# Other tables of places for the steps between the matmuls of a fused attention and bilinear GLU kernel

## The chip, the cores and the metric

The kernel runs on one core of one Trainium2 chip, in one launch. The metric is the device time of that launch in microseconds (us). Inputs are float32 in device memory, the output is float32.

## The reference

`x` is 2048 rows of 576 values. Attention has 32 heads of 18 values and a sliding window of 256 keys; the feed-forward part is a bilinear GLU of width 4608, whose output goes through a silu and gates the attention's output.

```python
xn = _layernorm(x)                                   # S = 2048, D = 576
q, k, v = split(xn @ wqkv)                           # H = 32 heads, Dh = 18
scores = einsum("bhqd,bhkd->bhqk", q, k) * Dh ** -0.5
scores = where((i - j >= 0) & (i - j < 256), scores, -1e9)
s = einsum("bhqk,bhkd->bhqd", softmax(scores), v).reshape(B, S, D) @ wo
h = (xn @ w_gate) * (xn @ w_up)                      # F = 4608, no nonlinearity
g = silu(h @ w_down)
return x + s * g
```

## The kernel before

**Numbers in two parts.** Every float32 operand of a matmul is held as two float16 tiles, a hi part and a low part (what the hi part leaves over, scaled), and a product is three matmuls: hi by hi, hi by low, low by hi. Most of the work between the matmuls is the making of these parts: ScalarE writes the hi part (`hi`, L190), VectorE the low part (`lo`, L193).

**Slots.** After a prologue (layer norm, the projections to q, k and v) the kernel runs 72 slots: 18 groups of 256 feed-forward columns, times 4 chunks of 512 rows. A slot is named by its group and chunk, so a group is four slots, and its first slot is the one that begins with new weights. In a slot TensorE computes the up and gate products of its chunk and group in a scheme of seven products of half blocks (`seven_place`, matmuls L1159 and L1112). Four of the seven use differences of weight blocks, which GpSimd makes (`t_sum`, L507, tile tf) and whose parts ScalarE and VectorE make (`t_hi`, `t_lo`, tile tw). The seven results are joined in tiles gt by ScalarE (`seven_copy`, L1125) and VectorE (`seven_add`, L1129), multiplied (`seven_mult`, L1134, on GpSimd for the first half, on VectorE for the second), and split into parts hh (`h_hi`, L1001, ScalarE; `h_lo`, L1007, VectorE). The down product of a slot (`down`, L1023, five of them, 0 to 4, each with a sum into acc on VectorE, L1030) runs in the slot after it, and takes six matmuls: for each half of h, hi by hi, hi by low, low by a copy of the down weight's hi part scaled down (`dn_low`, L605).

**Attention.** The slots from 1 to 64 carry one attention step each: two heads and four blocks of 128 queries (8 pairs of head and block, numbered 0 to 7; a block is 2i and 2i+1). Its stages are `score_pairs` (PE, L896), `score` (VectorE, L907, adds the mask and takes the maximum), `shifted` and `probs` (ScalarE, L915, L919; the second head's also copies the hi parts of P of both heads, L922), `turn_probs` (the low part of P, L928, on GpSimd or VectorE; the second head's then starts the DMA that transposes the block, L931, on SyncE's queue), `weigh` (PE, L940, the products with V), `finish` (VectorE, L952 and L953) and `finish2` (GpSimd, L960, L967, L968), then `store_o`.

**What sets the order.** A slot has 16 places. `seven_place` issues the up and gate matmuls of each; every other step is put by hand with `at(slot, place, f, ...)`, and a place of 16 or more means a place of the next slot. Within a place the scores' matmuls come first, down products second, the rest in the order in which the program puts it there. Each engine runs its steps in this order, so a step that waits holds up what stands behind it on its engine. All the places stand in one dictionary, `AT` (lines 68 to 106); the steps' code doesn't change. Its entries:

- `p`: for each slot of a group, for each of the 8 pairs, the places of score, shifted, probs, turn_probs and weigh. `end`: finish, finish2, store_o. `load`: the loads of k, q, v.
- `en`: for each slot of a group, from the third entry on, the engine of the low part of P of each pair (0 GpSimd, 1 VectorE). `eng`: of its entries two are read by steps, [4] (`dn_low`: 1 ScalarE, 0 GpSimd) and [5].
- `h`: the places of h_hi and h_lo for the two halves. `down`: the five down products. `dn`: parts of the down weights (hi, low, low copy).
- `raw`, `amax`, `scale`: loads and scales of the weights of a group; `up_hi`, `up_lo`, `wd`, `sum`, `t_hi`, `t_lo`: their parts and differences, counted from four slots ahead of the group (so 64 is place 0 of its first slot).
- `sx`, `on`, `t0`, `u0`, `g0`, `wd0`: the same kinds of steps for the first group, and sums of x, in the prologue and slot 0.

```python
(nc.gpsimd, nc.vector)[AT["en"][(s + 1) % NCH][2 + 2 * i + j]].tensor_tensor(...)   # turn_probs, L928
at(sl, AT["h"][sl % NCH][1][ft], h_lo, sl, ft)
at(sl + 1, AT["down"][(sl + 1) % NCH][n], down, sl, n)
```

Of the kernel before, what the change touches and what calls it, by code (L numbers as in the profile page):

```python
# [20 lines left out]
def kernel(  # L21
# [23 lines left out]
    scale = DH ** -0.5  # L45
# [19 lines left out]
    C_OUT = 1.0 / (XS * PROJ * WTOP * WTOP)  # L65
    LEAST, MOST = 2.0 ** -60, 2.0 ** 60

    AT = {"amax": (19, 20, 6),
           "dn": ((41, 45), (51, 52), (52, 48)),
           "down": ((6, 9, 12, 15, 20), (6, 8, 11, 14, 16), (6, 8, 11, 14, 16), (6, 9, 12, 15, 19)),  # L70
           "en": ((0, 1, 0, 0, 0, 0, 1, 0, 0, 0), (0, 1, 0, 0, 0, 0, 1, 0, 0, 0),
                  (0, 1, 0, 0, 0, 0, 1, 0, 0, 0), (0, 1, 0, 0, 0, 0, 1, 0, 0, 0)),
           "end": ((30, 32, 35), (28, 32, 33), (28, 32, 33), (28, 32, 33)),
           "eng": (1, 1, 0, 1, 1, 0, 1, 0, 0, 0, 0, 0, 0, 1),
           "g0": (-22, -19, -22, -21, -9, -16, -14, -11, -11),
           "h": (((15, 17), (18, 21)), ((15, 17), (19, 21)), ((15, 17), (21, 21)), ((15, 17), (19, 21))),
           "load": (8, 3, 15),
           "mult": {1: 6, 4: 18, 5: 1, 6: 0},
# [12 lines left out]
           "pairs": (6, 13),  # L91
           "raw": (8, 9, 12, 16, -6, 0),
           "scale": (26, 28, 35, 51),
           "sum": ((30, 36, 50, 59, 64), (41, 53, 56, 61, 62)),
# [5 lines left out]
           "t_hi": ((57, 57), (67, 69)),  # L100
           "t_lo": ((57, 58), (70, 71)),
           "u0": ((-9, -8, -7, -7), (-7, -7, -7, -4)),
           "up_hi": (36, 36, 60, 61),
           "up_lo": (41, 40, 65, 62),
           "wd": ((55, 56), (65, 69), (70, 74)),
           "wd0": ((-4, 3), (-1, 4), (-1, 7))}

    ctx.enter_context(tc.manual_schedule())
    const = ctx.enter_context(tc.tile_pool(name="const", bufs=1))
# [492 lines left out]
    def dn_low(g, k):  # L602
        w = DW[g, k]
        if AT["eng"][4]:
            nc.scalar.activation(w[:, 2], w[:, 0], AF.Copy, scale=1.0 / LO)  # L605
# [22 lines left out]
    def at(slot, place, f, *a):  # L628
        todo.setdefault(slot * 16 + place, []).append((f, a))
# [5 lines left out]
    for c in range(NCH):  # L635
        steps = s_steps(c)
        for n, f in enumerate(steps):
            for k, f in enumerate(f if isinstance(f, tuple) else (f,)):
                at(0, AT["sx"][c][n] + k, f, (nc.gpsimd, nc.vector)[AT["on"][c][n]])
    for k in range(3):  # L640
        at(0, AT["g0"][k], ffn_amax, 0, (2, 0, 1)[k])
    for k, f in enumerate((ffn_spread_out, ffn_spread_in, ffn_scale, ffn_scale2)):
        at(0, AT["g0"][5 + k], f, 0)
    for kind in range(2):
        for n in range(4):
            at(0, AT["t0"][kind][n], t_sum, 0, kind, n)
        for pair in range(2):
            at(0, AT["t0"][kind][4 + pair], t_hi, 0, kind, pair)
            at(0, AT["t0"][kind][6 + pair], t_lo, 0, kind, pair)
# [675 lines left out]
```

## Time and profile before

| | us |
|---|---|
| device time, median of 3 runs | 1578.68 |
| lowest and highest | 1578.66, 1579.19 |
| the profiled execution's own time | 1580.56 |
| its span in the trace | 1578.8 |
| granted clock of TensorE, mean | 0.999 of full speed |

| engine | busy us | share of the span |
|---|---|---|
| PE (TensorE matmul) | 1556.4 | 99% |
| DVE (VectorE) | 1268.3 | 80% |
| ACT (ScalarE) | 1069.4 | 68% |
| POOL (GpSimd) | 847.7 | 54% |

In the rows below, PE is TensorE's matmul, DVE VectorE, ACT ScalarE, POOL GpSimd. A row of a timeline has the start, the duration, the engine, the line, the operation and the tiles (out<-in) with partitions x elements; x6 at its end joins six instructions that follow each other, and a bracket names the idle time before it and what ended it. A duration runs from an instruction's start to its end, and holds what it waited for after its start. Successive rows of one engine overlap a little, since the next begins in the pipeline behind the one before; the net time of a step is the distance to the next row's start.

### The profile page before, as it was taken

Reading aid. Unit: us, or ns where it says so; the run is one execution under the profiler, and the core shown is the slowest. Engines: PE = TensorE matmul, PEld = TensorE weight load, DVE = VectorE, ACT = ScalarE, POOL = GpSimd, SP = SyncE. Lnnn points to the kernel's source line nnn. Section 1 sums busy time; section 2 is a strip of 40 time slices with the busy share of each in tenths; the row PEclk is TensorE's granted clock in tenths of the full one; section 3 lists DMA queues with packets and bytes.
Section 4 is the critical chain, followed back from the end, with each engine's and each line's share of the span. In section 5 each row is a group of like instructions: output and inputs, shape, how many; then the busy total and the mean of one; then the engine's idle time right before and its main releaser. Section 6 shows DMA issues by size and latency. Waiting matters only on the chain.

```text
span 1578.8 us, 40055 instructions
## 1 busy us (share of the span) xinstructions
PE 1556.4 (99%) x15498; PEld 1106.7 (70%) x15498; DVE 1268.3 (80%) x2752; ACT 1069.4 (68%) x1853; POOL 847.7 (54%) x1064
## 2 busy tenths in 40 slices
PE   8999999999999999999999999999999999999999
PEld 5465577777777776777777777777777777777767
DVE  7537688888888988898889888888888888877654
ACT  6435478777777877777778787878777777752230
POOL 4126355657464757575766666566757575732000
PEclk9999999999999999999999999999999999999999
DMA  9583436565557687777777676767686868651238
GB/s 233 190 246 129 166 73 138 96 129 107 122 106 143 122 146 137 130 143 135 145 122 152 121 155 119 154 121 149 118 158 123 155 120 149 122 98 38 63 82 220
DMA packets 566575, 212.14 MB, mean 134 GB/s; under 512 B 504560, under 2 KB 544624, under 8 KB 566384
## 3 DMA queue, kind: packets, MB, share of 16 engines
q1 hardware_dynamic: 566384, 209.58, 64.2%
q8 instruction: 121, 1.98, 0.6%
q14 instruction: 70, 0.57, 0.1%
HBM read 76.63 MB, written 29.00 MB: 67 GB/s over the span
## 4 chain that ended last, share of the span: by engine, by line
PE 83%; DVE 6%; POOL 4%; DMA 3%; ACT 2%; issue 2%; SPq 1%; DVEq 0%; POOLq 0%; ACTq 0%
PE up L1159 40%; PE dn L1023 21%; PE s L387 4%; PE pv L940 3%; PE up L1112 3%; PE s L896 2%; PE s L1023 2%; PE s L1262 2%; DMA pt<-pp 2%; PE up L1262 2%; PE up L387 1%; POOL pp L928 1%; DVE hh L1007 1%; POOL tf L507 1%; PE s L338 1%
## 5 line engine op out<-in xcount | busy, mean ns | idle before, releaser
L1023 PE MATMUL dn<-dnw,hh 128*128 128x512 f16 (+1 forms) x3168 | 444.7, 286 | 1.2
L1159 PEld LDWEIGHTS <-tw 128*128 128x128 f16 x3456 | 320.2, 98 | 62.1 <-DVE tw L193 5.1
L1023 PEld LDWEIGHTS <-hh 128*128 128x128 f16 x3456 | 222.2, 98 | 170.8 <-issue 19.2
L1159 PEld LDWEIGHTS <-upw 128*128 128x128 f16 x3024 | 283.8, 98 | 64.5 <-issue 22.2
L1129 DVE SCALAR_TENSOR_TENSOR gt<-up,gt 128x512 f32<-128x512 f32 x360 | 247.7, 688 | 62.4 <-PE up L1112 40.3
L1030 DVE SCALAR_TENSOR_TENSOR acc<-dn,sc,acc 128x512 f32<-128x512 f32 x310 | 215.3, 694 | 99.2 <-PE dn L1023 99.0
L1159 PE MATMUL up<-XT,upw 128*128 128x256 f16 x2160 | 276.6, 273 | 0.0
L915 ACT ACTIVATE mx<-mx,sig 128x2 f32<-128x2 f32 x256 | 98.1, 383 | 217.5 <-DVE mx L907 217.5
L1159 PE MATMUL up<-XT,tw 128*128 128x256 f16 x1728 | 236.0, 273 | 2.5 <-DVE gt L1129 2.5
L1159 PE MATMUL up<-sx,tw 128*128 128x256 f16 x1728 | 225.0, 273 | 2.4 <-DVE tw L193 2.4
L1134 POOL TENSOR_TENSOR ht<-gt 128x512 f32<-128x512 f32 x72 | 92.0, 1278 | 94.7 <-DVE gt L1129 93.9
L940 PEld LDWEIGHTS <-pt 128*128 128x128 f16 x2880 | 109.5, 96 | 41.1 <-DMA pt<-pp 6.3
L940 PE MATMUL pv<-vt,pt 128*128 128x37 f16 x2880 | 112.9, 179 | 4.5 <-DMA pt<-pp 4.5
L1159 PE MATMUL up<-sx,upw 128*128 128x256 f16 x864 | 112.7, 273 | 0.0
L1125 ACT ACTIVATE gt<-up 128x512 f32<-128x512 f32 x144 | 83.7, 581 | 30.9 <-PE up L1159 17.3
L1001 ACT ACTIVATE hh<-ht 128x512 f16<-128x512 f32 x72 | 45.2, 627 | 67.4 <-POOL ht L1134 67.4
L507 POOL TENSOR_TENSOR tf<-raw 128x256 f32<-128x256 f32 x102 | 83.0, 814 | 0.1
L507 POOL TENSOR_TENSOR tf<-raw,tf 128x256 f32<-128x256 f32 x68 | 62.0, 913 | 21.8 <-DVE tw L193 21.8
L193 DVE SCALAR_TENSOR_TENSOR upw<-raw,sc,upw 128x640 f16<-128x640 f32 x72 | 71.9, 1001 | 0.0
L315 ACT ACTIVATE upw<-raw 128x1280 bf16<-128x1280 f32 (+1 forms) x51 | 62.5, 1225 | 3.8 <-DMA raw<-in_B_w_up_dram 3.7
L193 DVE SCALAR_TENSOR_TENSOR tw<-tf,sc,tw 128x512 f16<-128x512 f32 x68 | 49.5, 749 | 14.5 <-ACT tw L190 13.7
L896 PE MATMUL s<-ks,qs 54*128 54x384 f16 (+2 forms) x512 | 60.2, 312 | 0.0
(1353 smaller groups left out, 2918.3 us busy)
## 6 DMA issues: line engine op xcount, KB each, us to landing
raw<-in_B_w_down_dram SPq DMA_DIRECT2D x36, 288.0 KB
qk_d<-qp SPq DMA_DIRECT2D x18, 512.0 KB
raw<-in_B_w_gate_dram SPq DMA_DIRECT2D x36, 256.0 KB
raw<-in_B_w_up_dram SPq DMA_DIRECT2D x36, 256.0 KB
ks<-qk_d SPq DMA_DIRECT2D x96, 81.0 KB
qs<-qk_d SPq DMA_DIRECT2D x128, 54.0 KB
vt<-v_d SPq DMA_DIRECT2D x48, 111.0 KB
qk_d<-qp SPq DMA_DIRECT2D x20, 256.0 KB
```

The lines of the kernel that those rows point to most:

```text
L193: nc.vector.scalar_tensor_tensor(w, rv, s, h, op0=OP.mult, op1=OP.subtract)
L387: nc.tensor.matmul(ps, a, b, start=i == 0 and not opened, stop=i == 12 and opened)
L507: nc.gpsimd.tensor_tensor(t[:, to], x0, x1, op=OP.subtract)
L896: nc.tensor.matmul(ps[:, :hi_ - lo_], QS[s][r, i * 128:(i + 1) * 128], KS[s][r, lo_:hi_], start=True, stop=True)
L915: nc.scalar.activation(mx[:, 1], mx[:, 0], AF.Identity, bias=sig[:, 2:3], scale=sig[:, 1:2])
L940: nc.tensor.matmul(PVB[s][:, j, i, :VW], pt[:, nb * j + n + n // nb * nb], VT[s][:, lo_ + n % nb, j * VW:(j + 1) * VW], start=n == 0, stop ...
L1023: nc.tensor.matmul(to, a, b, start=q == 0, stop=q == len(l) - 1)
L1030: nc.vector.scalar_tensor_tensor(d, src, SC[g][:, 9:10], d, op0=OP.mult, op1=OP.add)
L1125: nc.scalar.activation(seven_new(sl, name), CH[q], AF.Copy, scale=H_SC)
L1129: nc.vector.scalar_tensor_tensor(seven_new(sl, name), CH[q], H_SC, x, op0=OP.mult, op1=OP.add)
L1134: eng.tensor_tensor(HT[sl, f], u[:, 0], u[:, 1], op=OP.mult)
L1159: nc.tensor.matmul(CH[q][:, o], a, b, start=CH["first"], stop=last and q not in (1, 2, 5), skip_group_check=q in ON)
```

## The change

Only the tables change; each step computes what it did.

- The low part of P of pair 5 goes from GpSimd to VectorE in three of four slots (`en`, kinds 1 to 3: 48 instructions of 128x384). In slots of kind 0 pairs 4 and 5 change engines with each other.
- `dn_low` (36 instructions of 128x576) goes from ScalarE to GpSimd (`eng[4]`).
- `p` has a table of its own for each kind of slot: in kind 0 the first products with V stand up to three places earlier and those of pairs 4 and 5 one later, in kind 1 the products with V of pairs 2 to 7 two places later; low parts of P of pairs 4 and 5 in kind 2 one place earlier; `probs` of pairs 6 and 7 in kind 3 one place later, so in place 5 of a group's first slot.
- In a group's first slot, where steps of the slot before it spill: the fifth down product at place 2 and not 3 (`down` of kind 3: 18 for 19); `h_lo` of the first half at place 5 and not 3 (`h` of kind 3: 21 for 19), behind the small low part of `wd` that comes there from place 6; `t_hi` of the first pair at place 5 and not 3, behind `probs`. The fifth down product of kind 0 moves the other way, to place 5 of the second slot.
- `h`, `dn`, `sum`, `t_lo`, `up_hi`, `scale`, `load`, `raw`, `end` shift by one to seven places; steps of the prologue (`sx`, `on`, `t0`, `u0`, `g0`, `wd0`) shift, and three of its sums change engine.

```diff
--- before.py
+++ after.py
@@ -65,45 +65,45 @@
     C_OUT = 1.0 / (XS * PROJ * WTOP * WTOP)
     LEAST, MOST = 2.0 ** -60, 2.0 ** 60
 
-    AT = {"amax": (19, 20, 6),
-           "dn": ((41, 45), (51, 52), (52, 48)),
-           "down": ((6, 9, 12, 15, 20), (6, 8, 11, 14, 16), (6, 8, 11, 14, 16), (6, 9, 12, 15, 19)),
-           "en": ((0, 1, 0, 0, 0, 0, 1, 0, 0, 0), (0, 1, 0, 0, 0, 0, 1, 0, 0, 0),
-                  (0, 1, 0, 0, 0, 0, 1, 0, 0, 0), (0, 1, 0, 0, 0, 0, 1, 0, 0, 0)),
-           "end": ((30, 32, 35), (28, 32, 33), (28, 32, 33), (28, 32, 33)),
-           "eng": (1, 1, 0, 1, 1, 0, 1, 0, 0, 0, 0, 0, 0, 1),
-           "g0": (-22, -19, -22, -21, -9, -16, -14, -11, -11),
-           "h": (((15, 17), (18, 21)), ((15, 17), (19, 21)), ((15, 17), (21, 21)), ((15, 17), (19, 21))),
-           "load": (8, 3, 15),
-           "mult": {1: 6, 4: 18, 5: 1, 6: 0},
-           "on": ((0, 0, 0, 0, 1, 0, 1, 1, 1, 0, 0, 0, 0, 0, 1, 0, 1),
+    AT = {"amax": (18, 20, 6),
+           "dn": ((41, 45), (51, 55), (52, 48)),
+           "down": ((6, 9, 12, 15, 21), (6, 8, 11, 14, 16), (6, 8, 11, 14, 16), (6, 9, 12, 15, 18)),
+           "en": ((0, 1, 0, 0, 0, 0, 0, 1, 0, 0), (0, 1, 0, 0, 0, 0, 1, 1, 0, 0),
+                  (0, 1, 0, 0, 0, 0, 1, 1, 0, 0), (0, 1, 0, 0, 0, 0, 1, 1, 0, 0)),
+           "end": ((29, 31, 32), (30, 33, 35), (28, 32, 35), (28, 30, 33)),
+           "eng": (1, 1, 0, 0, 0, 0, 1, 0, 0, 0, 1, 0, 1, 1),
+           "g0": (-22, -21, -20, -18, -10, -17, -14, -11, -11),
+           "h": (((15, 17), (18, 19)), ((15, 19), (19, 21)), ((15, 17), (18, 21)), ((15, 17), (21, 21))),
+           "load": (7, 3, 13),
+           "mult": {1: 6, 4: 20, 5: 1, 6: 0},
+           "on": ((0, 0, 0, 1, 0, 0, 0, 1, 1, 0, 0, 0, 1, 0, 1, 0, 1),
                   (0, 1, 0, 1, 0, 0, 0, 1, 0, 0, 1, 0, 1, 1, 0, 0, 0),
-                  (1, 0, 0, 1, 0, 0, 1, 1, 1, 0, 1, 0, 1, 1, 1, 1, 1),
-                  (0, 0, 1, 0, 0, 1, 0, 0, 0, 0, 1, 1, 1, 1, 0, 0, 1)),
-           "p": (((6, 7, 8, 11, 22), (6, 7, 8, 12, 22), (7, 8, 12, 13, 22), (7, 8, 12, 13, 23),
-                  (13, 14, 15, 18, 24), (13, 14, 15, 19, 24), (13, 15, 20, 21, 30), (15, 17, 20, 21, 30)),
+                  (1, 0, 0, 1, 0, 0, 1, 1, 1, 0, 1, 0, 1, 1, 1, 0, 1),
+                  (0, 0, 1, 0, 0, 1, 1, 0, 0, 0, 1, 1, 0, 1, 0, 0, 0)),
+           "p": (((6, 7, 8, 10, 19), (6, 7, 9, 12, 20), (7, 8, 12, 13, 21), (7, 8, 12, 13, 22),
+                  (13, 14, 15, 18, 25), (13, 14, 15, 19, 25), (13, 15, 20, 21, 29), (15, 17, 20, 21, 29)),
+                 ((6, 7, 8, 11, 22), (6, 7, 8, 12, 22), (7, 8, 10, 13, 24), (7, 8, 10, 13, 25),
+                  (13, 14, 15, 18, 26), (13, 14, 15, 19, 26), (13, 15, 20, 21, 30), (15, 17, 20, 21, 30)),
+                 ((6, 7, 8, 11, 22), (6, 7, 8, 12, 22), (7, 8, 12, 14, 22), (7, 8, 12, 14, 23),
+                  (13, 14, 15, 16, 25), (13, 14, 15, 18, 25), (13, 15, 20, 21, 28), (15, 17, 20, 21, 28)),
                  ((6, 7, 8, 11, 22), (6, 7, 8, 12, 22), (7, 8, 12, 13, 22), (7, 8, 12, 13, 23),
-                  (13, 14, 15, 18, 24), (13, 14, 15, 19, 24), (13, 15, 20, 21, 28), (15, 17, 20, 21, 28)),
-                 ((6, 7, 8, 11, 22), (6, 7, 8, 12, 22), (7, 8, 12, 13, 22), (7, 8, 12, 13, 23),
-                  (13, 14, 15, 17, 26), (13, 14, 15, 19, 26), (13, 15, 20, 21, 28), (15, 17, 20, 21, 28)),
-                 ((6, 7, 8, 11, 22), (6, 7, 8, 12, 22), (7, 8, 12, 13, 22), (7, 8, 12, 13, 23),
-                  (13, 14, 15, 19, 26), (13, 14, 15, 20, 26), (13, 15, 20, 22, 28), (15, 17, 20, 22, 28))),
+                  (13, 14, 15, 19, 26), (13, 14, 15, 20, 26), (13, 15, 21, 22, 28), (15, 17, 21, 22, 28))),
            "pairs": (6, 13),
-           "raw": (8, 9, 12, 16, -6, 0),
-           "scale": (26, 28, 35, 51),
-           "sum": ((30, 36, 50, 59, 64), (41, 53, 56, 61, 62)),
+           "raw": (7, 9, 16, 17, -6, -2),
+           "scale": (26, 28, 35, 50),
+           "sum": ((32, 39, 46, 59, 66), (43, 53, 56, 61, 62)),
            "sx": ((-24, -24, -24, -23, -22, -22, -18, -18, -17, -17, -14, -13, -13, -19, -18, -17, -14),
                   (-20, -20, -20, -18, -17, -16, -16, -16, -16, -15, -13, -13, -9, -15, -15, -15, -12),
                   (-13, -11, -11, -9, -7, -7, -3, -3, 2, 3, 4, 5, 6, 4, 6, 7, 14),
-                  (-4, -1, -1, 6, 8, 9, 11, 12, 14, 15, 16, 16, 24, 23, 26, 26, 26)),
-           "t0": ((-19, -9, -7, -7, -6, -2, -5, -1), (-11, -8, -4, -7, -4, -2, -1, -1)),
-           "t_hi": ((57, 57), (67, 69)),
-           "t_lo": ((57, 58), (70, 71)),
-           "u0": ((-9, -8, -7, -7), (-7, -7, -7, -4)),
-           "up_hi": (36, 36, 60, 61),
+                  (-4, -1, -1, 6, 8, 9, 11, 12, 14, 15, 16, 19, 24, 23, 26, 26, 26)),
+           "t0": ((-14, -10, -8, -7, -6, -2, -5, -1), (-10, -8, -4, -6, -4, -2, -1, -1)),
+           "t_hi": ((57, 57), (69, 70)),
+           "t_lo": ((57, 57), (70, 71)),
+           "u0": ((-8, -7, -7, -3), (-7, -7, -6, -1)),
+           "up_hi": (37, 37, 61, 61),
            "up_lo": (41, 40, 65, 62),
-           "wd": ((55, 56), (65, 69), (70, 74)),
-           "wd0": ((-4, 3), (-1, 4), (-1, 7))}
+           "wd": ((55, 56), (65, 71), (69, 74)),
+           "wd0": ((-2, 2), (-1, 4), (-1, 7))}
 
     ctx.enter_context(tc.manual_schedule())
     const = ctx.enter_context(tc.tile_pool(name="const", bufs=1))
```

## Rows read from the trace of the kernel before

**Rows 1.** The page: busy us of TensorE, and its granted clock in tenths.

```profile
PE 1556.4 (99%) x15498; PEld 1106.7 (70%) x15498; DVE 1268.3 (80%) x2752; ACT 1069.4 (68%) x1853; POOL 847.7 (54%) x1064
PEclk9999999999999999999999999999999999999999
```

**Rows 2.** Windows: stretch, busy us of each engine (instructions), clock, DMA share, GB/s.

```profile
493.00:1403.00 910.00, 901.91 (x9803) 656.20 (x9802) 786.96 (x1723) 711.53 (x1199) 586.04 (x709) 1.00 0.73 136
```

**Rows 3.** Chain of waits in order of time: start us, us, what.

```profile
493.40 1.64 PE up L1159 x15
...
1024.99 1.64 PE up L1159 x15
...
1043.64 1.64 PE up L1159 x15
...
1100.57 1.54 PE up L1159 x14
...
1402.99 1.64 PE up L1159 x15
```

**Rows 4.** Waits of TensorE: line, releaser, us in total, times, longest.

```profile
PE pv L940 <- DMA pt<-pp: 4.5, 5, 1.1
PE up L1159 <- DVE gt L1129: 2.5, 2, 2.1
PE up L1159 <- DVE tw L193: 2.4, 8, 0.4
```

**Rows 5.** Timeline of TensorE, first slot of a group.

```profile
1076.29 1.75 PE L1023 MATMUL dn<-dnw,hh 128*128 128x512 f16 x6
```

**Rows 6.** Timeline of VectorE, the same slot.

```profile
1074.11 0.48 DVE L1030 SCALAR_TENSOR_TENSOR acc<-dn,sc,acc 128x256 f32<-128x256 f32 x1 [0.27 <-PE dn L1023]
1074.51 1.12 DVE L928 TENSOR_TENSOR pp<-sm__17355,pp 128x384 f16<-128x384 f32 x1
1075.55 1.40 DVE L1007 SCALAR_TENSOR_TENSOR hh<-hh,ht 128x512 f16<-128x512 f16 x1
1076.87 0.68 DVE L1007 SCALAR_TENSOR_TENSOR hh<-hh,gt 128x512 f16<-128x512 f16 x1
```

**Rows 7.** Timeline of GpSimd, the same slot.

```profile
1074.08 0.45 POOL L968 TENSOR_TENSOR ob<-o,ob 128x144 f16<-128x144 f32 x1
1074.49 0.73 POOL L507 TENSOR_TENSOR tf<-raw 128x256 f32<-128x256 f32 x1
1075.17 1.23 POOL L928 TENSOR_TENSOR pp<-sm__17355,pp 128x384 f16<-128x384 f32 x1
```

**Rows 8.** Timeline of ScalarE, the same slot.

```profile
1075.25 0.72 ACT L190 ACTIVATE tw<-tf,sc 128x512 f16<-128x512 f32 x1 [0.69 <-POOL tf L507]
1075.88 1.29 ACT L919 ACTIVATE sm__17359<-sm__17359,mx,sig 128x384 f32<-128x384 f32 x2
1077.20 0.83 ACT L922 CAST pp<-sm__17359 128x768 f16<-128x768 f32 x1
```

**Rows 9.** Groups of instructions by form: busy us, mean ns; idle before, releasers.

```profile
L605 ACT ACTIVATE dnw<-dnw 128x576 f16<-128x576 f16 x36 | 24.2, 673 | 0.0
L967 POOL CAST ob<-o 128x144 f16<-128x144 f32 x64 | 25.0, 391 | 4.2
L268 POOL TENSOR_TENSOR xh<-xn,xh 128x512 f16<-128x512 f32 x15 | 17.4, 1158 | 0.1
```

**Rows 10.** Timeline of VectorE, a low part of P while GpSimd is idle.

```profile
396.35 0.54 DVE L928 TENSOR_TENSOR pp<-sm__5455,pp 128x384 f16<-128x384 f32 x1
```

**Rows 11.** Timelines of VectorE and TensorE, fourth slot of a group.

```profile
1132.55 0.68 DVE L1007 SCALAR_TENSOR_TENSOR hh<-hh,gt 128x512 f16<-128x512 f16 x1
1133.22 1.47 PE L1023 MATMUL dn<-dnw,hh 128*128 128x512 f16 x6
```

**Rows 12.** Timeline of TensorE, a wait for transposed P.

```profile
627.00 0.47 PE L940 MATMUL pv<-vt,pt 128*128 128x37 f16 x12 [1.04 <-DMA pt<-pp]
```

**Rows 13.** Timeline of TensorE, down products of the last slots.

```profile
1501.07 1.04 PE L1023 MATMUL s<-dnw,hh 128*128 128x512 f16 x4 [0.19 <-DVE hh L1007]
```

## The prediction

> **What bounds the kernel now.** I read the shares and the clock line of the page first. PE is busy 99% of the span and its clock stands at full speed [rows 1], so the time is that of the matmuls plus whatever makes PE wait. The windows then say how much waiting there is: from 493 to 1403 us PE is busy 901.91 of 910.00 us [rows 2]. Some 8 us of waiting there, and small gaps whose ends are modelled, are all that a reordering can win in that stretch.
>
> The chain of waits puts a place to it. One and the same piece of a slot, the 15 up matmuls of 1.64 us, comes back 18.65 us later where nothing waits (1024.99 to 1043.64). Four such slots are 74.60 us, but the group takes 75.58 (1024.99 to 1100.57). Twelve groups, from 493.40 to 1402.99, take 909.59 us [rows 3], which is 14.4 more than 12 x 74.60 = 895.2. By the waits of PE, 4.5 us of that are five waits of the products with V for a transposed P, and 2.4 are eight waits for a low part of a weight difference (tw); the third row, 2.5 us for gt, is one wait of 2.1 in the first slot of all and one of 0.4 at the end [rows 4]. The other 14.4 - 4.5 = 9.9 us are 0.82 a group.
>
> Now one group, whose first slot begins at 1070.48. The six down matmuls of 1076.29 take 1.75 us [rows 5]; the same six in another slot take 1.47 [rows 11]. So 0.28 us are a wait, and VectorE tells for what: its steps there are the sum of the fifth down product (which waits 0.27 us for PE), the low part of P (1.12), and the low parts of h, 1.40 and 0.68, ending at 1077.55 [rows 6]. The third of the six matmuls needs the first low part of h, at 1076.29 + 2 x 0.215 = 1076.72, the sixth needs the second, at about 1077.37. The rest of the 0.98, about 0.7, is the wait for tw in the same slot (mean 0.3 [rows 4]) and gaps around gt too short for a row.
>
> Why 1.40, and why 1.12? VectorE's low part of P takes 0.54 us where GpSimd is idle [rows 10], and its low part of h takes 0.68 there [rows 11]. In this slot they begin while a GpSimd step runs: P's at 1074.51, under one from 1074.49 to 1075.22; h's at 1075.55, under one from 1075.17 to 1076.40. Both end about 0.5 after that GpSimd step does [rows 6, 7]. So a VectorE step from SBUF to SBUF and a GpSimd step take turns: who comes second waits for the other's end. That turn-taking carries the forecast.
>
> **The change, slot by slot.** It takes no matmul away. It moves 48 low parts of P (one a slot in three of four) from GpSimd to VectorE and 36 low copies of the down weights from ScalarE to GpSimd, and it reorders the rest.
>
> First slot of a group, VectorE (times of the group above). The fifth down product stands a place earlier, so its sum no longer waits 0.27 for PE and is done at 1074.2. Then the fifth low part of P, of the step of the slot before: GpSimd's last step of the output runs to 1074.53 [rows 7], so it ends at 1074.53 + 0.42 = 1074.95 (0.42 being what a step takes once the other has gone: it ends 1075.63, 0.41 after 1075.22 [rows 6, 7]). GpSimd's weight difference of 0.73 has been waiting, runs 0.6 net to 1075.54, and P's sixth low part, new here, ends 0.42 later at 1075.96. GpSimd has nothing then, so the small low part that now stands ahead of h's takes 0.33 (1076.29), and h's first takes 0.68: 1076.97. That is 0.25 after its matmul wants it.
>
> Meanwhile ScalarE. Before, its exponentials stood behind the hi part of tw, which waited 0.69 us for GpSimd and took PE's slot time with it; the pair of exponentials and the copy run from 1075.88 to 1078.03 [rows 8]. Now that part stands behind them, the exponentials begin right after the step that ended at 1074.56, and the copy is done 1.3 earlier or a little more, 1076.61 to 1076.71. So GpSimd's seventh low part of P, which before began at 1078.1, behind h's, asks at about 1076.7, while h's first still runs to 1076.97. By the turn-taking it goes next: 0.78 net, 1077.75, and h's second ends 0.55 to 0.6 later, 1078.3. The sixth matmul wanted that at 1077.37: a wait of about 1.0 in all where there was 0.28.
>
> What comes back: tw's wait of 0.3 and its gaps go, since VectorE has two steps less between the scores and tw and ScalarE's part for it comes earlier against PE, which is itself 0.7 later; 0.1 to 0.2 remain around gt. Together 1.0 + 0.2 = 1.2 a group, against 0.98 here and 0.82 on the mean.
>
> The Trainium skill ("SBUF — State Buffer", section "SBUF: two separate sides") states that VectorE and GpSimd share one port pair as an exclusive lock, held for a whole instruction by whoever starts first. The rows just read agree (1.40 against 0.68), and by that rule a low part moved to VectorE is not out of GpSimd's way: it speaks against this change.
>
> The waits for transposed P (4.5 us): one is 1.04 us at 627.00 [rows 12]. They fall on the transposes issued after the sixth low part. This now ends at 1075.96 and not behind GpSimd's step at 1076.40 [rows 7], half a microsecond earlier, and PE comes 0.7 later: 1.2 more slack; for the attention step of the first slot itself, the products with V stand one place later in the table. I take 4 of the 4.5 as gone.
>
> Second to fourth slot. In the second and third the moved steps keep their order against the steps that PE takes its operands from; I take nothing there. In the fourth the low copies of the down weights now meet VectorE. They took 0.67 us on ScalarE. On GpSimd no row shows them: the nearest rows are 0.39 us for a cast of 128x144 and 1.16 for a step of 128x512 [rows 9]; the operation is a one-input one like the first but of four times the size, so I take 0.6 (ends 0.4 and 1.2). There h's second low part is done at 1133.23 and its matmul wants it at 1133.22 + 5 x 0.215 = 1134.3 [rows 11], a cover of about 1.1 us. After the change, a second low part of P (0.45) and one copy (0.6) use 0.9 or so: no wait at 0.6, up to 0.5 at 1.2. It is free only under that cover.
>
> By the skill's page "GPSIMD Engine Reference" (section "3.1 Elementwise — side-by-side cycle accounting") a one-input step costs 1.03 cycles an element; an estimate from that is 0.5 us for 576, which would leave the sum as it is.
>
> Ends. The last down products wait 0.19 and more for h [rows 13], which stands earlier in that slot kind: -0.6 at most with what follows. In the first slot of all, PE waits 2.1 us for gt [rows 4]; the prologue's steps moved between VectorE and GpSimd cost it 0 to +1.0, I take +0.3. The early groups, whose attention steps are shorter, show no wait in this slot and keep none.
>
> **The sum.** Twelve groups at 1.2 are 14.4, against 14.4 now with the DMA waits in it: 12 x (1.2 - 0.82) = +4.6, DMA -4.0 (4.5 with 0.5 left), tail -0.6, first slot +0.3, and -0.5 for slots where a DMA wait had been hiding part of the others: about -0.2. The profiled execution took 1580.56 us for a span of 1578.8; the median of the runs shown is 1578.68, 1.9 below it. What I worked out are differences of that execution, and I set them against the median: 1578.5. Its own range is 3 us to either side.
>
> **The rivals.** (1) h's second low part gets ahead. What decides is whether the seventh low part of P asks (1076.7) before h's first ends (1076.97), a margin of 0.28 us. If VectorE keeps the turn, or the copy comes 0.3 later, h is complete at 1077.57 as before, the group loses 0.4 and not 1.2, and P's low part goes behind it at no cost. 12 x (0.4 - 0.82) = -5.0, DMA -4, tail -0.6: 1569. For it: GpSimd's pair at 1078.1 did come behind h in the kernel before. Against it: there it was not ready.
>
> (2) Slower: the fourth slot. If the low copy on GpSimd is nearer 1.2 us than 0.6, or both copies fall between h's two low parts, the cover of 1.1 us is used up and down waits 0.5 a group more: 12 x 0.5 = +6, 1584.5. It decides from a copy of about 0.8 us on. For it: every GpSimd step of [rows 7] that met a VectorE step stretched. Against it: the copies are spread over two places, far from each other.
>
> (3) That the tables do nothing of the kind (the steps stay in the old order for want of data) would give 1578.7, within the forecast's range.
>
> **Chances.** Forecast 0.45, rival 1 0.28, rival 2 0.24, and 0.03 for something in the prologue, which the forecast's 0.3 us hardly covers. 0.2% is 3.2 us, about what a measurement can tell from no change: of the forecast's 0.45, 0.05 fall faster and 0.02 slower; with the rivals, faster 0.34, same 0.40, slower 0.26. The range reaches to both rivals, 1569 to 1584.5, since leaving out either would leave out more than 2 in 10.
>
> **What would show it.** Right: the six down matmuls of a group's first slot take 2.4 to 2.5 us and not 1.75; the second low part of h there takes 1.3 to 1.4 beside a GpSimd low part of P; PE's waits for transposed P fall under 1 us and those for tw vanish; the low copy on GpSimd lasts about 0.6. Wrong: the down matmuls keep 1.75 or less (rival 1), or six down matmuls of the fourth slot take 1.9 (rival 2), or PE's wait at the first slot grows past 3 us.

## The result and the profile after

The changed kernel takes 1585.91 us (median of 6 runs, 1585.37 to 1586.76), the kernel before 1578.90 (median of 6, 1578.66 to 1579.39): 7.0 us slower, ratio 1.0043 with an interval of 1.0033 to 1.0053. The forecast was 1578.5, and the range ended at 1584.5.

The page of the changed kernel, the lines that answer to [rows 1], and its window that answers to [rows 2]:

```profile
span 1583.5 us, 39928 instructions
PE 1557.8 (98%) x15498; PEld 1105.9 (70%) x15498; DVE 1292.5 (82%) x2798; ACT 1049.5 (66%) x1817; POOL 870.2 (55%) x1054
...
493.00:1403.00 910.00, 901.88 (x9788) 655.33 (x9786) 805.23 (x1764) 698.77 (x1177) 601.67 (x696) 1.00 0.74 136
```

Work moved as announced: VectorE has 24 us more, ScalarE 20 less. In the stretch from 493 to 1403 us PE is as busy as in the profile of [rows 2], to 0.03 us, so most of the loss against that profile lies outside this stretch. TensorE's waits (line, releaser, us in total, times, longest), to be read against [rows 4]:

```profile
PE dn L1023 <- DVE hh L1007: 8.4, 26, 0.5
PE up L1159 <- DVE gt L1129: 5.0, 8, 2.9
...
PE s L1023 <- DVE hh L1007: 1.7, 1, 1.7
```

The waits for transposed P and for tw are gone from this execution; in their place stand 26 waits of the down matmuls for the low part of h.

Where the time went is seen best in the lengths of the slots, from the first up matmul of one to that of the next. The four early groups are those that begin with slots 4, 8, 12 and 16, the twelve groups those that begin with slots 20 to 64. The second profile of the kernel before is one of the experiments below.

| | before, 1st profile | before, 2nd profile | after |
|---|---|---|---|
| slots 0 and 1 | 31.34 | 31.34 | 32.64 |
| first slots of the four early groups, mean | 18.21 | 18.21 | 18.93 |
| first slots of the twelve groups, sum | 237.43 | 235.84 | 238.90 |
| their median | 19.63 | 19.62 | 19.88 |
| the stretch of slots 17 to 64 (twelve groups) | 909.62 | 906.94 | 910.07 |
| slot 71 to the end of the last matmul | 80.87 | 80.87 | 81.27 |

Against the second profile the loss is 1.3 in slots 0 and 1, 4 x 0.72 = 2.9 in the early groups, 3.1 in the twelve, 0.4 at the end: 7.7 us, about what the medians show. Against the first profile the twelve groups look even, and the two spans (1578.8 and 1583.5) are only 4.7 apart: that execution of the kernel before was one of its long ones.

The first slot of the group that [rows 5 to 8] show, in the changed kernel (VectorE, GpSimd, ScalarE, TensorE):

```profile
1077.54 1.79 DVE L928 TENSOR_TENSOR pp<-sm__17353,pp 128x384 f16<-128x384 f32 x2
1079.36 0.35 DVE L193 SCALAR_TENSOR_TENSOR wd<-raw,sc,wd 64x128 f16<-64x128 f32 x1
1079.74 0.69 DVE L1007 SCALAR_TENSOR_TENSOR hh<-hh,ht 128x512 f16<-128x512 f16 x1
1080.35 1.40 DVE L1007 SCALAR_TENSOR_TENSOR hh<-hh,gt 128x512 f16<-128x512 f16 x1
...
1077.87 1.04 POOL L507 TENSOR_TENSOR tf<-raw 128x256 f32<-128x256 f32 x1
1080.07 2.46 POOL L928 TENSOR_TENSOR pp<-sm__17357,pp 128x384 f16<-128x384 f32 x2 [1.16 <-ACT pp L922]
...
1079.16 0.83 ACT L922 CAST pp<-sm__17357 128x768 f16<-128x768 f32 x1
...
1079.74 0.60 PE L1023 MATMUL dn<-dnw,hh 128*128 128x512 f16 x2
1080.49 0.82 PE L1023 MATMUL dn<-dnw,hh 128*128 128x512 f16 x3 [0.15 <-DVE hh L1007]
1081.81 0.39 PE L1023 MATMUL dn<-dnw,hh 128*128 128x512 f16 x1 [0.50 <-DVE hh L1007]
```

The copy on ScalarE ends at 1079.99, GpSimd's seventh low part of P asks at 1080.07, while VectorE's first low part of h runs to about 1080.4. GpSimd goes next, and h's second takes 1.40 where it took 0.68 [rows 6]. This is what is called the collision below. The down matmul that needs it is the last of the six, which begins at 1081.81, 2.07 after the first; without a wait that is 5 x 0.215 = 1.08. So the wait is 0.99.

The same slot of an early group shows the same order:

```profile
326.22 0.69 DVE L1007 SCALAR_TENSOR_TENSOR hh<-hh,ht 128x512 f16<-128x512 f16 x1
326.83 1.41 DVE L1007 SCALAR_TENSOR_TENSOR hh<-hh,gt 128x512 f16<-128x512 f16 x1
...
326.69 2.31 POOL L928 TENSOR_TENSOR pp<-sm__4175,pp 128x384 f16<-128x384 f32 x2 [3.96 <-ACT pp L922]
...
328.29 0.39 PE L1023 MATMUL dn<-dnw,hh 128*128 128x512 f16 x1 [0.21 <-DVE hh L1007]
...
329.08 0.60 PE L1159 MATMUL up<-XT,tw 128*128 128x256 f16 x4 [0.21 <-DVE gt L1129]
```

GpSimd asks at 326.69, 0.14 before h's second begins. And slot 0 (TensorE, GpSimd, VectorE), with the low copies of the down weights by form (busy us, mean ns):

```profile
186.40 2.72 PE L1159 MATMUL up<-XT,tw 128*128 128x256 f16 x12 [2.86 <-DVE gt L1129]
191.12 1.47 PE L1159 MATMUL up<-XT,tw 128*128 128x256 f16 x12 [0.59 <-DVE gt L1129]
...
180.60 3.41 POOL L607 TENSOR_SCALAR dnw<-dnw 128x576 f16<-128x576 f16 x2 [14.94 <-ACT dnw L190]
...
180.61 1.27 DVE L193 SCALAR_TENSOR_TENSOR dnw<-raw,sc,dnw 128x576 f16<-128x576 f32 x1
...
L607 POOL TENSOR_SCALAR dnw<-dnw 128x576 f16<-128x576 f16 x36 | 61.5, 1709 | 14.9 <-ACT dnw L190 14.9
```

A low copy takes 1.71 us on GpSimd. In slot 0 two of them run beside VectorE's low parts of the down weights, and the wait for gt is 2.86 where it was 2.11.

### The profile page after: what moved, and what is told of

Same layout as the page of the kernel before. It is cut to its first block, busy times and chain, and to the rows that moved or that the text cites. A ratio compares the mean times of both kernels' runs of the same rounds, so it can differ in the third digit from the quotient of the medians.

```text
span 1583.5 us, 39928 instructions
## 1 busy us (share of the span) xinstructions
PE 1557.8 (98%) x15498; PEld 1105.9 (70%) x15498; DVE 1292.5 (82%) x2798; ACT 1049.5 (66%) x1817; POOL 870.2 (55%) x1054
## 4 chain that ended last, share of the span: by engine, by line
PE 78%; DVE 15%; issue 3%; ACT 3%; DMA 1%; POOL 0%; SPq 0%; DVEq 0%; POOLq 0%; ACTq 0%
PE up L1159 36%; PE dn L1023 20%; PE pv L940 4%; PE s L387 4%; PE up L1112 2%; DVE hh L1007 2%; PE s L1023 2%; PE s L896 2%; DVE acc L1030 2%; PE s L1262 2%; DVE upw L193 2%; DVE pp L928 2%; PE up L1262 2%; DVE gt L1129 1%; PE up L387 1%
## 5 line engine op out<-in xcount | busy, mean ns | idle before, releaser
L1159 PE MATMUL up<-XT,tw 128*128 128x256 f16 x1728 | 229.2, 273 | 5.0 <-DVE gt L1129 5.0
L1159 PE MATMUL up<-sx,tw 128*128 128x256 f16 x1728 | 230.8, 273 | 0.0
L940 PEld LDWEIGHTS <-pt 128*128 128x128 f16 x2880 | 114.6, 96 | 40.1 <-issue 5.0
L940 PE MATMUL pv<-vt,pt 128*128 128x37 f16 x2880 | 120.7, 180 | 0.0
L507 POOL TENSOR_TENSOR tf<-raw 128x256 f32<-128x256 f32 x102 | 103.0, 1010 | 0.5 <-DVE sc L447 0.5
L607 POOL TENSOR_SCALAR dnw<-dnw 128x576 f16<-128x576 f16 x36 | 61.5, 1709 | 14.9 <-ACT dnw L190 14.9
L507 POOL TENSOR_TENSOR tf<-raw,tf 128x256 f32<-128x256 f32 x68 | 57.2, 842 | 18.0 <-DVE tw L193 17.9
L1007 DVE SCALAR_TENSOR_TENSOR hh<-hh,ht 128x512 f16<-128x512 f16 x72 | 65.8, 914 | 0.6
```

The lines of the kernel that those rows point to most:

```text
L507: nc.gpsimd.tensor_tensor(t[:, to], x0, x1, op=OP.subtract)
L940: nc.tensor.matmul(PVB[s][:, j, i, :VW], pt[:, nb * j + n + n // nb * nb], VT[s][:, lo_ + n % nb, j * VW:(j + 1) * VW], start=n == 0, stop ...
L1007: nc.vector.scalar_tensor_tensor(b, a, -LO, h, op0=OP.mult, op1=OP.add)
L1159: nc.tensor.matmul(CH[q][:, o], a, b, start=CH["first"], stop=last and q not in (1, 2, 5), skip_group_check=q in ON)
```

## The experiments

The theory after the result: the steps moved are harmless; what costs 7 us is that GpSimd's seventh low part of P now asks for its turn a few tenths too early and runs between h's two low parts. The rivals: that the added low part on VectorE makes h late, or that the low copies on GpSimd do. Each ratio below is to the kernel before as timed beside that run (medians of 1577.6 to 1578.9 us), and differences from the changed kernel are read from the ratios (its own is 1.0043). The lengths of slots are of one execution each.

**A second profile of the kernel before.**

> The kernel before, unchanged, profiled a second time. Theory: its waits for transposed P (five, 4.5 us, in the first profile) come and go from one execution to the next, so this profile shows other slots and a sum of 0 to 3 us, and the first slot of a group without one is again 19.63 us long. Rival: they are fixed, the same slots show 4.5 us again.

Its waits for transposed P:

```profile
PE pv L940 <- DMA pt<-pp: 1.9, 4, 0.5
```

1577.61 us, and 1.9 us of waits where [rows 4] have 4.5; by the slot lengths they cost only 0.3 us here (first slots of 19.76, 19.72, 19.64 and 19.62), since the wait for tw behind such a wait is gone: the four first slots that wait for transposed P are the four that don't wait for tw. In the first profile they cost 2.9 (first slots of 20.21, 19.86, 20.28 and 19.95, and one second slot of 19.75 where 18.65 is usual). So they come and go. A first slot without one is 19.62 again, but for one in each profile that waits 0.4 for tw and is 19.75.

**The small low part behind h's.**

```diff
-           "wd": ((55, 56), (65, 71), (69, 74)),
+           "wd": ((55, 56), (65, 71), (70, 74)),
```

> The changed kernel with one number put back: the small low part wd (0.35 us) stands behind the two low parts of h in a group's first slot, not ahead of them. Theory (GpSimd's seventh low part of P gets its turn between h's two low parts only because h's first is late by a few tenths): the first low part starts 0.35 us earlier, the second gets its turn first, the wait of the six down matmuls falls from 0.98 to 0.3 or less, in the four early groups from 0.73 to 0; up to 0.4 us a group come back as a wait for tw, behind the small low part. 9 to 12 us faster than the changed kernel: 1574 to 1577. What speaks against it within the theory: the margin is under 0.1 us. Rival (the wait is that of the one more low part of P on VectorE, whatever the order): second low part still ends about as late as it does, no more than 2 us gained.

1574.19 us, ratio to the kernel before 0.9976 (0.9967 to 0.9985): 11 us faster than the changed kernel, by one number. VectorE, GpSimd and TensorE in the first slot of the same group:

```profile
1072.93 0.68 DVE L1007 SCALAR_TENSOR_TENSOR hh<-hh,ht 128x512 f16<-128x512 f16 x1
1073.53 0.68 DVE L1007 SCALAR_TENSOR_TENSOR hh<-hh,gt 128x512 f16<-128x512 f16 x1
...
1076.64 0.35 DVE L193 SCALAR_TENSOR_TENSOR wd<-raw,sc,wd 64x128 f16<-64x128 f32 x1
...
1073.75 2.11 POOL L928 TENSOR_TENSOR pp<-sm__17357,pp 128x384 f16<-128x384 f32 x2 [1.16 <-ACT pp L922]
...
1073.41 1.47 PE L1023 MATMUL dn<-dnw,hh 128*128 128x512 f16 x6
...
1079.46 0.61 PE L1159 MATMUL up<-sx,tw 128*128 128x256 f16 x4 [0.20 <-DVE tw L193]
```

h's second begins 0.22 before GpSimd asks, takes 0.68, and the six down matmuls take 1.47. The wait for tw is back behind the small step, 0.2. First slots of a group are 19.17 long, those of the early groups 18.21 as before the change. The rival that the order doesn't matter falls. By slot lengths the collision costs 12 x 0.71 + 4 x 0.72 = 11.4 us, more than the 7.0 that the change lost: without it the changed kernel is 4 us faster than the one before, with 5.4 gained in the twelve first slots (19.62 to 19.17) and 1.3 + 0.4 lost in slots 0 and 1 and at the end.

**The exponentials later.**

```diff
-           "t_hi": ((57, 57), (69, 70)),
+           "t_hi": ((57, 57), (67, 69)),
```

> The changed kernel with the hi part of tw put back ahead of the last exponentials of P on ScalarE, so that GpSimd's seventh low part of P is ready 1.1 us later; VectorE's order stays as changed. Theory (turn-taking): both low parts of h run with no GpSimd step between them, the wait of the down matmuls falls from 0.98 to about 0.3 a group (0.73 to 0 to 0.1 in the early groups): 16 groups, 10 to 11 us faster than the changed kernel, about 1575. Rival (VectorE's own work, one low part of P and the small one more ahead of h, makes it late): the wait stays at 0.7 or more, under 4 us gained.

1574.56 us, 0.9977 (0.9969 to 0.9986). VectorE's order is that of the changed kernel; only GpSimd's step is ready later (VectorE, GpSimd, TensorE):

```profile
1072.06 0.69 DVE L1007 SCALAR_TENSOR_TENSOR hh<-hh,ht 128x512 f16<-128x512 f16 x1
1072.67 0.68 DVE L1007 SCALAR_TENSOR_TENSOR hh<-hh,gt 128x512 f16<-128x512 f16 x1
...
1074.13 1.79 POOL L928 TENSOR_TENSOR pp<-sm__17357,pp 128x384 f16<-128x384 f32 x2 [2.90 <-ACT pp L922]
...
1072.07 1.78 PE L1023 MATMUL dn<-dnw,hh 128*128 128x512 f16 x6
```

What is left is the 0.31 us by which h's first is late (1.78 for the six down matmuls against 1.47): 19.20 a first slot, early ones 18.21. Two different edits take the same 0.7 us a group away, and both do it by the same order of the two steps. That the collision is the cause of the loss in the sixteen first slots is shown.

**The low copies back on ScalarE.**

```diff
-           "eng": (1, 1, 0, 0, 0, 0, 1, 0, 0, 0, 1, 0, 1, 1),
+           "eng": (1, 1, 0, 0, 1, 0, 1, 0, 0, 0, 1, 0, 1, 1),
```

> The changed kernel with the low copies of the down weights back on ScalarE. Theory: on GpSimd they took 1.7 us each, but cost PE only in the first slot of all (there two of them stretch VectorE's low parts of the down weights by 0.85 us ahead of gt): about 1 us faster, 1585. Rival (second rival of the prediction): they make h late in every fourth slot or shift GpSimd's work into the first: 4 to 7 us faster.

1585.71 us, 1.0047 (1.0033 to 1.0061) of the kernel before, against 1.0043 for the changed kernel: no difference that can be measured. The rival falls: the twelve first slots are 19.88 with them and without, every fourth slot 18.65. Slots 0 and 1 are 31.31 here and not 32.64; 0.75 of that is the shorter wait for gt, the rest changes from one execution to the next (see slot 0 below). But the early first slots became 19.10 long and not 18.93, and the last slot 0.3 longer. Why ScalarE's extra steps do that there wasn't tried.

**The low parts of P back on GpSimd, places as changed.**

```diff
-           "en": ((0, 1, 0, 0, 0, 0, 0, 1, 0, 0), (0, 1, 0, 0, 0, 0, 1, 1, 0, 0),
-                  (0, 1, 0, 0, 0, 0, 1, 1, 0, 0), (0, 1, 0, 0, 0, 0, 1, 1, 0, 0)),
+           "en": ((0, 1, 0, 0, 0, 0, 1, 0, 0, 0), (0, 1, 0, 0, 0, 0, 1, 0, 0, 0),
+                  (0, 1, 0, 0, 0, 0, 1, 0, 0, 0), (0, 1, 0, 0, 0, 0, 1, 0, 0, 0)),
```

> The changed kernel with the engines of P's low parts as before (48 back on GpSimd), all places as changed. Theory (turn-taking decides, not who does the work): on GpSimd the sixth low part takes its turn between the small low part wd and h's first, and the seventh between h's two, so h's second ends as late as in the changed kernel: the down wait stays near 1.0 us a group, within 3 us of the changed kernel (1583 to 1588). Rival (the low part moved onto VectorE is what makes h late): the wait falls to 0.5 or less, 7 to 11 us faster.

1593.87 us, 1.0095 (1.0079 to 1.0110): 8 us slower than the changed kernel, so the rival is refuted, and the theory's 3 us were too small too. Its mechanism is there (VectorE, GpSimd, a group's first slot):

```profile
1085.03 1.29 DVE L1007 SCALAR_TENSOR_TENSOR hh<-hh,ht 128x512 f16<-128x512 f16 x1
1086.25 1.40 DVE L1007 SCALAR_TENSOR_TENSOR hh<-hh,gt 128x512 f16<-128x512 f16 x1
...
1084.81 0.96 POOL L928 TENSOR_TENSOR pp<-sm__17353,pp 128x384 f16<-128x384 f32 x1
1086.01 2.42 POOL L928 TENSOR_TENSOR pp<-sm__17357,pp 128x384 f16<-128x384 f32 x2 [0.23 <-ACT pp L922]
...
1070.43 0.56 DVE L907 CUSTOM_DVE_ANT_0 sm__17222<-s,bias 128x384 f32<-128x384 f32 x1 [0.84 <-POOL pp L928]
...
1073.19 0.92 PE L1159 MATMUL up<-XT,tw 128*128 128x256 f16 x7 [0.52 <-DVE gt L1129]
```

Both low parts of h wait for a turn, and the first slot stays at 19.80. What I hadn't in the sum is the fourth slot: with one step more on GpSimd, its low parts of P end later, VectorE's next score waits 0.84 for one of them to free its tile, and gt is 0.5 late. Fourth slots are 19.32 and not 18.65, which is 8.0 us in twelve of them; the early first slots are 1.8 longer in sum (19.39 each), the twelve first slots 1.2 and slots 0 and 1 0.6 shorter. So in the changed kernel's places the moved low part is worth 8 us.

**That move alone, in the kernel before.**

```diff
-           "en": ((0, 1, 0, 0, 0, 0, 1, 0, 0, 0), (0, 1, 0, 0, 0, 0, 1, 0, 0, 0),
-                  (0, 1, 0, 0, 0, 0, 1, 0, 0, 0), (0, 1, 0, 0, 0, 0, 1, 0, 0, 0)),
+           "en": ((0, 1, 0, 0, 0, 0, 0, 1, 0, 0), (0, 1, 0, 0, 0, 0, 1, 1, 0, 0),
+                  (0, 1, 0, 0, 0, 0, 1, 1, 0, 0), (0, 1, 0, 0, 0, 0, 1, 1, 0, 0)),
```

> The kernel before with the engines of P's low parts alone changed. Theory: h's first low part no longer meets GpSimd's sixth low part of P (0.68 in place of 1.40), the sixth comes between h's two, which are complete 0.3 us earlier: the 0.28 us wait of the down matmuls goes in the twelve groups, while the transposes of that block are issued some 0.3 later and wait a little more: 0 to 4 us faster than before. Rival (one more step on the busier engine costs): 2 to 6 us slower.

1575.89 us, 0.9982 (0.9974 to 0.9991): 3.0 us faster than before. VectorE in a group's first slot, and TensorE's waits for transposed P:

```profile
1071.78 0.68 DVE L1007 SCALAR_TENSOR_TENSOR hh<-hh,ht 128x512 f16<-128x512 f16 x1
1072.38 0.55 DVE L928 TENSOR_TENSOR pp<-sm__17355,pp 128x384 f16<-128x384 f32 x1
1072.85 0.68 DVE L1007 SCALAR_TENSOR_TENSOR hh<-hh,gt 128x512 f16<-128x512 f16 x1
...
PE pv L940 <- DMA pt<-pp: 5.1, 6, 1.3
```

h's first low part takes 0.68 where it took 1.40 [rows 6], and the wait for h is gone. A first slot without a late transpose is 19.32 long. The waits for transposed P are 5.1 us; as the kernel before had 4.5 in one execution and 1.9 in another, that they grew is not shown. The rival falls.

**Four steps moved at once.**

```diff
-           "eng": (1, 1, 0, 0, 0, 0, 1, 0, 0, 0, 1, 0, 1, 1),
+           "eng": (1, 1, 0, 0, 1, 0, 1, 0, 0, 0, 1, 0, 1, 1),
-           "t_hi": ((57, 57), (69, 70)),
+           "t_hi": ((57, 57), (67, 69)),
-           "wd": ((55, 56), (65, 71), (69, 74)),
+           "wd": ((55, 56), (65, 71), (72, 74)),
-            at(sl, (17, 18)[ft] if last else AT["h"][sl % NCH][1][ft], h_lo, sl, ft)
+            at(sl, (17, 17)[ft] if last else AT["h"][sl % NCH][1][ft], h_lo, sl, ft)
```

> The changed kernel with the hi part of tw ahead of the exponentials, the small low part wd three places later (behind h and tw), the low copies of the down weights on ScalarE, and h's second low part of the last slot ahead of the sum there. Theory: the twelve groups lose 0.2 to 0.4 us each and not 1.24, the early ones nothing, slot 0 is back at the length of before less 0.5, the last slot loses 0.4 less: 1568 to 1571, some 8 faster than before. Rival (the small steps put back come late in another place): no better than 1574.

1577.85 us, 0.9992 (0.9984 to 1.0001). No gain on the kernel before, as the rival had it, and the rows name the place (VectorE, GpSimd, TensorE):

```profile
1077.97 1.29 DVE L193 SCALAR_TENSOR_TENSOR tw<-tf,sc,tw 128x512 f16<-128x512 f32 x1
1080.92 0.35 DVE L193 SCALAR_TENSOR_TENSOR wd<-raw,sc,wd 64x128 f16<-64x128 f32 x1
...
1076.92 1.80 POOL L928 TENSOR_TENSOR pp<-sm__17357,pp 128x384 f16<-128x384 f32 x2 [2.89 <-ACT pp L922]
...
1082.04 0.93 PE L1159 MATMUL up<-XT,tw 128*128 128x256 f16 x7 [0.49 <-DVE gt L1129]
```

h is in time (1.47 for the six down matmuls), but GpSimd's pair, later now, meets the low part of tw: 1.29 where it takes 0.75, and the small step behind the second low part of tw stands ahead of gt, which is 0.49 late. The end gained 1.5 us (79.73 for 81.27), the twelve first slots are 19.71.

**The same with the low parts of P back on GpSimd.** To the run above:

```diff
-           "en": ((0, 1, 0, 0, 0, 0, 0, 1, 0, 0), (0, 1, 0, 0, 0, 0, 1, 1, 0, 0),
...
+           "en": ((0, 1, 0, 0, 0, 0, 1, 0, 0, 0), (0, 1, 0, 0, 0, 0, 1, 0, 0, 0),
...
```

> The same with the 48 low parts of P back on GpSimd. Theory: GpSimd's sixth low part again takes its turn ahead of h's first, which costs 0.3 to 0.5 us a group: 4 to 6 us slower than with them on VectorE. Rival (the low parts' engine makes no difference, only the order of the rest does): within 1.5 us of it.

1578.11 us, 0.9994 (0.9985 to 1.0003): the same as with them on VectorE, so here the rival holds. Whether that step is worth 8 us, 3 us (in the kernel before) or nothing hangs on the places around it.

**The exponentials later, and the two ends.**

```diff
-           "eng": (1, 1, 0, 0, 0, 0, 1, 0, 0, 0, 1, 0, 1, 1),
+           "eng": (1, 1, 0, 0, 1, 0, 1, 0, 0, 0, 1, 0, 1, 1),
-           "t_hi": ((57, 57), (69, 70)),
+           "t_hi": ((57, 57), (67, 69)),
-            at(sl, (17, 18)[ft] if last else AT["h"][sl % NCH][1][ft], h_lo, sl, ft)
+            at(sl, (17, 17)[ft] if last else AT["h"][sl % NCH][1][ft], h_lo, sl, ft)
```

> The changed kernel with the hi part of tw ahead of the exponentials, the low copies of the down weights on ScalarE, and h's second low part of the last slot ahead of the sum there; the small low part wd stays ahead of h. Theory (the wait for a turn goes to whichever VectorE step from SBUF is late when GpSimd's pair of low parts of P starts): the group's first slot stays at 19.2 us, since PE is 0.3 us behind tw there, and the last slot loses 1.5 less: 1570 to 1573. Rival (the low copies on ScalarE make h late, which cost 0.17 a group in the early ones when h was late already): 1575 or more.

1573.07 us, 0.9970 (0.9959 to 0.9982). First slots 19.20, the end 79.71, as the theory had it; early first slots 18.39 and not 18.21, which is the 0.17 a group that the rival named, though not its total.

**The small step last, and the two ends.**

```diff
-           "eng": (1, 1, 0, 0, 0, 0, 1, 0, 0, 0, 1, 0, 1, 1),
+           "eng": (1, 1, 0, 0, 1, 0, 1, 0, 0, 0, 1, 0, 1, 1),
-           "wd": ((55, 56), (65, 71), (69, 74)),
+           "wd": ((55, 56), (65, 71), (74, 74)),
-            at(sl, (17, 18)[ft] if last else AT["h"][sl % NCH][1][ft], h_lo, sl, ft)
+            at(sl, (17, 17)[ft] if last else AT["h"][sl % NCH][1][ft], h_lo, sl, ft)
```

> The changed kernel with the small low part wd behind h, tw and the next gt (five places later than in the changed kernel), with the low copies on ScalarE and the last slot's order as in the run above. Theory: GpSimd's pair of low parts of P runs beside the scores, whose source is PSUM and which take no turns, h and tw are both in time, and the first slot of a group falls to 18.8 to 19.0: 1567 to 1571, the fastest of all. Rival: the small part meets GpSimd later and makes a matmul of the slot's end late; no better than with wd right behind h (19.17).

1571.65 us, 0.9961 (0.9947 to 0.9974) of the kernel before, the fastest: 13 us under the changed kernel. First slots are 18.86 (VectorE's tw, GpSimd's pair):

```profile
1072.99 0.75 DVE L193 SCALAR_TENSOR_TENSOR tw<-tf,sc,tw 128x512 f16<-128x512 f32 x1
...
1070.20 2.11 POOL L928 TENSOR_TENSOR pp<-sm__17357,pp 128x384 f16<-128x384 f32 x2 [1.16 <-ACT pp L922]
```

GpSimd's pair runs from 1070.20 to 1072.31, beside the sums and scores, which read PSUM and take 0.74 and 0.55 as always; it is done before tw's low part begins. Waits for transposed P are left (2.4 us), and 0.9 for tiles gt that ScalarE writes, in second slots. In this execution they took back what the first slots gained: the stretch of slots 17 to 64 is 901.73, against 901.96 with the small part right behind h. So what this run gains on that one (0.9961 against 0.9976) lies by the slot lengths in slots 0 and 1 (0.75) and at the end (1.5).

## Why the prediction was wrong

- **The first slot of a group: right.** The wait of about 1.0 us for h came as 0.99, by the steps as they were worked out: GpSimd's request at 0.08 after the copy, 0.28 ahead of the start of h's second and 0.36 ahead of the end of its first (forecast: 0.28), h's second at 1.40. The price of 1.2 for a group, over four slots of 18.65, came as 1.23 (19.88 - 18.65). The waits for tw went, as forecast.
- **The early groups: one of the two costliest misses.** "Show no wait in this slot and keep none" was read from the rows of before, and the new order wasn't worked through there. It is the same order and the same collision; 4 x 0.72 = 2.9 us, where the sum has nothing.
- **The DMA waits: a credit that wasn't there.** 4.0 us were taken off because one execution showed 4.5. They did go in the changed kernel's execution, but even in the first profile they cost 2.9 us and not 4.5, and a second execution of the kernel before loses 0.3 us by them. The step that failed is taking a sum over twelve groups (14.4 us) from the one profiled execution, although it lay 1.9 us above the median, and taking the waits off it in full. The 0.82 a group that was left for the other waits was too small by that: a first slot without a late transpose costs 19.62 - 18.65 = 0.97. So the twelve groups, +4.6 - 4.0 - 0.5 = +0.1 in the sum, came to 12 x (1.23 - 0.97) = +3.1.
- **The low copy on GpSimd: mis-sized.** Taken at 0.6, ends 0.4 and 1.2, it lasts 1.71 us, outside the bounds. The step was called one of four times the size of a row of 0.39 us, and was still taken at 0.6; in proportion to size that row gives 1.6 (an estimate from [rows 9]). An estimate from the Trainium skill ("GPSIMD Engine Reference", section "3.1 Elementwise — side-by-side cycle accounting") was 0.5 us, by its 1.03 cycles an element, a figure that names neither this operation nor 16-bit values; the measurement is 3.4 times that, and the measurement decides. It still cost nothing in the fourth slot (18.65), and the cover of 1.1 us that was to pay for it was not called on: in the fourth slots from 19 to 63 the copies run beside VectorE's sums, scores and joins of gt, which read PSUM, and none runs beside a low part of h. So the second rival, which had the right size of the total (1584.5), is not what happened; that its total was near is luck.
- **Slot 0: +1.3, not +0.3.** Of that, 0.75 is the longer wait for gt (2.86 for 2.11), which is gone in each run with the copies on ScalarE. The rest comes and goes: with the same tables for slots 0 and 1 the run with the exponentials later has 32.09 where the changed kernel has 32.64, and of those with the copies on ScalarE and the changed places some have 31.3 and some 31.9. What changes it stays open.
- **The end: +0.4, not -0.6.** The fifth down product of the last but one slot, a place earlier, put its sum (1522.64) ahead of h's second low part on VectorE, and the down matmuls wait:

```profile
1522.64 0.48 DVE L1030 SCALAR_TENSOR_TENSOR acc<-s,sc,acc 128x256 f32<-128x256 f32 x1
1523.03 0.68 DVE L1007 SCALAR_TENSOR_TENSOR hh<-hh,gt 128x512 f16<-128x512 f16 x1
...
1523.77 1.47 PE L1023 MATMUL s<-dnw,hh 128*128 128x512 f16 x6 [1.66 <-DVE hh L1007]
```

  The kernel before had h's second ahead of that sum, and a wait of 1.27 there. With the changed kernel's places and h's second ahead of the sum, the end takes 79.7 us.
- **The first rival** named the point that decides (0.28 us, who asks first) and priced the other outcome at 0.4 a group. The edits that tip it gave 19.17 - 18.65 = 0.5 and 11 us less.

In one line: the mechanism and its price were right for twelve groups; the four early groups, slots 0 and 1 and the end were judged by the rows of before (forecast -0.3 in sum, measured +2.9, +1.3 and +0.4), and a gain of 4.0 was booked from waits that the second execution of the kernel before hardly shows.

## What to carry to other kernels

Where two engines take turns, what a step costs can hang more on when it asks than on how long it is: here a step of 0.35 us, one place further on, was worth 11 us, and copies of 1.7 us cost nothing in the fourth slots. Before moving a step, list for each step that a matmul waits for which step of the other engine can ask in the half microsecond ahead of it, and put the other one's work beside steps that read PSUM. Work a new order through in every kind of stage, also in those that show no wait now. And don't book as a gain a wait that depends on a transfer's moment unless a second execution shows it too.

## What the runs showed of the hardware

- VectorE and GpSimd took turns: a GpSimd step that asked 0.14 to 0.28 us before VectorE's second step from SBUF was due got the next turn between two VectorE steps that were ready back to back, in the twelve groups and the four early ones alike (the second took 1.40). One that asked 0.22 us after the second step's begin came behind it (0.68).
- VectorE's steps that read PSUM took as long beside GpSimd's low parts of P as alone: scores 0.55, sums 0.75, joins of gt 0.69.
- A scaled copy of 128x576 from f16 to f16 took 1.64 to 2.24 us on GpSimd, median 1.66, where ScalarE took 0.67.
- Two of these copies (3.41 us) beside VectorE's low parts of the down weights stretched those to 1.27 and 1.21 only, from 0.81. The first of them ended at 181.88, and the copy beside it, which began at 180.60 and took 1.64 at least, at 182.24 or later. So this step did not wait for the copy's end, while those in [rows 6] that met a GpSimd step of [rows 7] ended 0.4 to 0.6 after it.
